# A fused transformer block: waits at the ramp, at the end of attention and in the last stage, and the order of the work around them

## The chip, the cores and the metric

The kernel runs on one core of one Trainium2 chip. The time is the device time of one execution in microseconds; three runs were made, and the median counts. The profile is of one execution of its own.

## The reference

One transformer block with its two branches in parallel, on x of 2048 tokens by 640 (float32). The normalised x feeds the windowed attention and the gated branch, and both are added to x.

```python
xn = layernorm(x)                                   # 2048 x 640
q, k, v = split(xn @ wqkv)                          # 32 heads of 20
scores = q @ k.T * 20 ** -0.5                       # only 0 <= query - key < 256
A = softmax(scores) @ v, heads joined, @ wo
B = (gelu(xn @ w_gate) * (xn @ w_up)) @ w_down      # 1728 wide
out = x + A + B
```

## The kernel before, in words

A product of two float32 matrices is made as three products of their rounded upper and lower parts (`h` and `l` in the names: xh, xl, wqh, wql). ScalarE copies the upper part, and VectorE or GpSimd subtracts it from the raw value for the lower part. A "dense" tile of 128 features by 512 tokens is so 15 matmuls of 128x128 by 512 columns (`dense_steps`, L106).

**Ramp.** Each of the four chunks of 512 tokens is normalised, transposed on TensorE (L184) and split into xh (ScalarE, L192) and xl (VectorE, L193). Before the last chunk's transposes are all copied out, attention's first maxima begin: `attention` (L802) runs twelve steps ahead of its first unit, which pull pairs of maxima on every second step and eight dense matmuls on each.

**Attention.** It goes over 32 units: a unit is four heads (a group) by one chunk of 512 queries, with 14 slots (`NS`) each. `max_pair` (L472, matmuls ps_m L491, row maxima on VectorE L501) finds the maxima that the softmax subtracts; it takes two PSUM banks of a pool of four, which the transposes of the ramp use too. `exp_piece` (L542) makes scores (ps_e, L556) and their exponentials P on ScalarE (L558), in six pairs on the odd slots 1 to 11. `clear` (L564) lets GpSimd zero the parts of P outside the window (the selects, L571 and L574). In slot 0 of the next unit `av_unit` (L577) multiplies P by V (ps_o, L599, 96 short matmuls in the trace), ScalarE copies the two halves out (L605, L606) and GpSimd adds them (L609). `load_stack` (L457) loads a unit's queries and keys (qs, ks, L466) from DRAM three units ahead.

Between these, TensorE gets dense matmuls from a generator, `filler` (L689): `pull_fill(n)` adds n to a debt and issues matmuls until it is paid. Each slot pulls RATE / NS. The generator goes through `sets` in their order: ("qk", i) is one weight tile for queries and one for keys for all four chunks, ("gu", f) one tile of gate and up; V of the second half of the heads comes in between at a given slot. Each q/k tile is saved in three bfloat16 parts with a step on ScalarE, VectorE and GpSimd (L276, L272, L254, L258) and stored to DRAM (L267).

```python
RATE = 31.2                                                              # L32
...
    sets = [("qk", 1), ("qk", 2), ("qk", 3), ("gu", 0), ("qk", 4)]       # L684
    sets += [("gu", f) for f in range(1, NFA)] + [("gu", NF - 1)]
...
        for u in range(NU + 1):                                          # attention
            for i in range(NS):
...
                if i == 0 and u:
                    av_unit(u - 1)
                    flush()
                    pull_max(2, T)
...
                pull_fill(RATE / NS)
```

**Gate phase.** The other tiles of gate and up (L864 `gate_up`, L931 `gate_up_pair`, ps_g L106 and L949) run on sums of two chunks, which need fewer products. `w_tiles` (L898) splits the weights, the lower parts on GpSimd (wql, L99 and L881).

**Last stage.** P is done; the down projection and the output projection run as eight pairs of 128 tokens (p), each of ten steps (k and "e"). In step n the program loads the activations of step n + 4 (`load_step`), splits those of step n + 2 (`split_step`, L1145: ScalarE L1162 and L1170, VectorE by the helper of L1054), does what `plan` has for n (`prepare`, L1402) and then issues the step's matmuls (ps, L1216, `terms`). In `plan`, "f" fetches a weight quad (on ScalarE's queue, L1020), "h" makes its upper part (ScalarE, L1035) and "l" its lower one (VectorE, L1054); "b" is a quad as it is, "t" one of sums. `drain` (L1234) adds finished PSUM banks into the output (xr, L1239).

**Order.** Each engine takes its instructions in order. In attention the order of TensorE, ScalarE, VectorE and GpSimd is the written one (`manual_schedule`), SyncE's is a scheduler's. In the gate phase (L1294) TensorE, ScalarE, VectorE and SyncE follow the written order, GpSimd the scheduler's. The last stage has all five written. Where two phases meet, the work of the later one can stand among that of the earlier one.

Of the kernel before, what the change touches and what calls it, by code (L numbers as in the profile page):

```python
# [28 lines left out]
SR = 3 * DH  # L29
QROWS = 64 + SR  # L30
NS = 14
RATE = 31.2  # L32
V1_SLOT = 169
MXD = 7
KSLOT = 9
# [9 lines left out]
RAMP = 4.0  # L45
GAP = 16
VW = 1408
MANUAL_OUT = {mybir.EngineType.SP}
MANUAL = {mybir.EngineType.PE, mybir.EngineType.Activation, mybir.EngineType.DVE}
# [17 lines left out]
def block_kernel(ctx, tc, x, wqk, wv, wgu, wdo, wdl, out):  # L67
# [129 lines left out]
    now = [None]  # L197

    def at(slot, fn, *a):
        acts.setdefault(slot, []).append((fn, a))  # L200
# [9 lines left out]
    def flush():  # L210
        while lates:
            fn, a = lates.pop(0)
            fn(*a)
# [4 lines left out]
    def defer(n, fn, *a):  # L218
        if now[0] is None:
            fn(*a)  # L220
        else:
            at(now[0] + n, fn, *a)
# [109 lines left out]
    def run(*gens):  # L332
        for gen in gens:
            for _ in gen:
                pass
# [121 lines left out]
    def load_stack(u, which=(0, 1)):  # L457
        g, c = divmod(u, NC)
        for m in range(80 * g // 128, (80 * g + 79) // 128 + 1):
            assert all((m + 5 * i, c) in done for i in which), (u, m)  # L460

        for i in which:
            dst, src, top, again = ((qs[u % NQ], qd[c], 1, 2), (ks[u % NK], kd[c], 0, 0))[i]
            for j in (0, 2):
                for p, part, n in ((j * 32, top, 2), (j * 32 + 2 * DH, again, 1), (64 - j * 32, 0, 3)):
                    nc.sync.dma_start(dst[p:p + DH * n, j:j + 2].rearrange("p j t -> p (j t)"),  # L466
                                      src[g, part:part + n].rearrange("s (d j) t -> (s d) (j t)",
                                                                      j=4)[:, j * C:(j + 2) * C])
# [54 lines left out]
    def pieces(c):  # L523
        b = 4 * c
        X = [(b, 0, 0, 384)] + ([(b - 2, 384, 0, 128)] if c else [])
        Y = [(b + 1, 0, 128, 384), (b + 3, 384, 384, 128)]
        Z = ([(b - 1, 0, 0, 256)] if c else []) + [(b + 2, 256, 256, 256)]
        return X, Z, Y
# [48 lines left out]
    def av_unit(u):  # L577
        g, c = divmod(u, NC)
        v = vtiles[g]
        os = [psx.tile([128, C], F32, name="ps_o", tag="ex") for _ in range(2)]  # L580
        place = {kb - 4 * c: (pts[u, bi], col, q0) for bi, bank in enumerate(pieces(c)) for kb, col, q0, n in bank}

        def half(d, r):
            i = 2 * d + r
            return d, r, max(0, 64 * i), min(C, 64 * i + 320)

        steps_ = [((0, 0), (0, 1)), ((2, 0), (-1, 1)), ((-1, 0), (2, 1)), ((1, 0), (1, 1)),
                  ((3, 0), (-2, 1)), ((-2, 0), (3, 1))]
        todo = [half(*x) for pair in steps_ for x in pair if x[0] in place]
        begun_, left = set(), [sum(t[1] == r for t in todo) for r in range(2)]  # L590
        for d, r, qa, qb in todo:
            pt, col, q0 = place[d]
            kb = 4 * c + d
            assert (id(v), kb) in done, (u, kb)
            left[r] -= 1
            rows = slice(64 * r, 64 * r + 64)
            for j in range(4):
                w0_ = kb * 84 + 21 * j
                nc.tensor.matmul(os[r][32 * j:32 * j + 32, qa:qb], v[rows, w0_:w0_ + 32],  # L599
                                 pt[rows, j, col + qa - q0:col + qb - q0], start=r not in begun_,  # L600
                                 stop=not left[r], skip_group_check=True, tile_position=(64 * r, 32 * j))
            begun_.add(r)
        ob, oc = ap.tile([128, C], F32, name="ob", tag="ob", bufs=1), pts[u, 2][:, 0]
        lo = 0 if c else 64
        nc.scalar.activation(ob, os[0], AF.Copy)  # L605
        nc.scalar.activation(oc[:, lo:], os[1][:, lo:], AF.Copy)  # L606

        def join():
            nc.gpsimd.tensor_tensor(out=ob[:, lo:], in0=ob[:, lo:], in1=oc[:, lo:], op=OP.add)  # L609

        def store():
            for j in range(4):
                nc.sync.dma_start(od[c].rearrange("(d h) t -> h d t", h=H)[4 * g + j], ob[32 * j:32 * j + DH, :])
            nc.sync.dma_start(sd[c][4 * g:4 * g + 4, :], ob[DH::32, :])

        defer(3, join)
        defer(5, store)
# [63 lines left out]
                                   lambda k: xh[:, k, cs], lambda k: xl[:, k, cs], KT)  # L681
            defer(1, *((late, c4) if i else (c1,)))

    sets = [("qk", 1), ("qk", 2), ("qk", 3), ("gu", 0), ("qk", 4)]  # L684
    sets += [("gu", f) for f in range(1, NFA)] + [("gu", NF - 1)]
    pools = (wp, None), (hp, 2)
    rest = []
# [91 lines left out]
    NU = NG * NC  # L779
    stream = ((u, i) for u in range(NU) for i in range(8))  # L780
    fill = filler()
    debt = [0.0]

    def pull_max(n, slot):
        for _ in range(n):
            x = next(stream, None)
            if x is None:
                return
            max_pair(*x)
            if x[1] == 7:  # L790
                at(slot + (MXD if slot >= 0 else 4), max_end, x[0])

    def tick():
        todo = [y for t in sorted(t for t in acts if t <= now[0]) for y in acts.pop(t)]
        return sorted(todo, key=lambda y: y[0] is max_end)

    def pull_fill(n):
        debt[0] += n
        while debt[0] > 0:
            debt[0] -= next(fill, 1.0)  # L800

    def attention():  # L802
        now[0] = -1
        load_stack(0)
        load_stack(1)
        load_stack(2)
        for i, (p, k, half) in enumerate((p, k, half) for p in range(NC // 2) for k in range(2) for half in range(2)):
            for j, fn in enumerate(x_sums(p, k, half)):
                m = 10 * i + j
                at(NS * (XS0 + m // XSN) + m % XSN, fn)  # L810
        for i in range(12):
            now[0] = i - 13
            for fn, a in tick():
                fn(*a)
            if i % 2 == 0:
                pull_max(2, now[0])
            flush()
            pull_fill(2 * RAMP)
        pull_fill(GAP)
        for u in range(NU + 1):  # L820
            for i in range(NS):
                T = now[0] = NS * u + i
                for fn, a in tick():
                    fn(*a)
                if i in (0, 5, 9) or T == 3:
                    pull_max(2, T)
                if i == 0 and u:
                    av_unit(u - 1)
                    flush()
                    pull_max(2, T)  # L830
                if i % 2 and i < 12 and u < NU:
                    exp_piece(u, i - 1)
                    if i == 1 and u:
                        pull_fill(1)
                        debt[0] -= 1
                    exp_piece(u, i)
                flush()
                if u + 3 < NU and i in (KSLOT, 12):
                    load_stack(u + 3, (int(i == KSLOT),))
                pull_fill(RATE / NS)  # L840
        while acts:
            now[0] += 1
            for fn, a in tick():
                fn(*a)
            flush()
        now[0] = None
        run(fill)
        assert not acts

    with tc.manual_schedule(engines=MANUAL | {mybir.EngineType.Pool}):  # L850
        attention()
# [439 lines left out]
        nc.sync.dma_start(t, x[256 * p:256 * p + 256].rearrange("(a p) d -> p a d", a=2))  # L1291
        return t

    order = tc.manual_schedule(engines=MANUAL_OUT | MANUAL)  # L1294
    order.__enter__()
    raws_w = load_gu(NFA)
    banks = [psg.tile([128, C], F32, name="ps_g", tag=f"g{i}") for i in range(4)]
# [34 lines left out]
    for j, f in enumerate(range(NFA, NF - 1)):  # L1332
# [50 lines left out]
        if not end:  # L1383
            w = nxt_w[0], sums
    order.__exit__(None, None, None)
    order = tc.manual_schedule(engines=MANUAL_OUT | MANUAL | {mybir.EngineType.Pool})
# [9 lines left out]

    plan = {1: "hb4 lb4", 2: "hb5 lb5", 3: "hb6 lb6 s4", 4: "fb7 ht4 lt4", 5: "fb8 s5", 6: "hb7 ht5 lb7 lt5",
            7: "ft6 ft8 hb8 lb8", 8: "ft7 ht6 lt6", 9: "ft0 ht8", 10: "lt8 ht7 lt7", 11: "ft1 ft2 ht0 lt0",
            12: "ft3 ht1 lt1", 15: "p20", 16: "p21", 17: "p22", 18: "p23", 22: "p30", 23: "p31", 25: "p32",
            26: "p33"}  # L1400

    def prepare(n):  # L1402
# [24 lines left out]
    for n, (p, k) in enumerate(steps):  # L1427
        i = n % (NQD + 1)
# [71 lines left out]
```

## Time and profile before

| | us |
|---|---|
| median of 3 runs | 1049.95 |
| lowest, highest run | 1048.82, 1053.6 |
| the profiled execution | 1055.0 |
| its span, first to last instruction | 1053.2 |

The profile is of one execution, so its durations are held against its own 1055.0. An engine's busy time counts its instructions and not the waits between them; PE is TensorE, PEld its weight loads, DVE VectorE, ACT ScalarE, POOL GpSimd, SP SyncE. A row of the timeline gives start and duration in us, engine, line, operation, output <- inputs, shape, count, and in brackets the idle time before it and what ended it. In rows of windows stands the granted clock of TensorE, 1.00 at full speed.

### The profile page before, as it was taken

The page shows a single profiled execution, that of the slowest core. Times are in us where ns is not written, and L with a number is a line of the kernel's source. Part 1 is how long each engine was busy: PE and PEld are TensorE (multiplying, and loading weights), DVE is VectorE, ACT ScalarE, POOL GpSimd, SP SyncE. Part 2 cuts the span into 40 slices and gives each one's busy share as a digit, 9 for nine tenths or more (in the row PEclk, how much of TensorE's full clock was granted, in tenths as well). Part 3 has the DMA queues.
Part 4 walks back from the last instruction along what each step waited for, and adds up shares of the span by engine and source line. Part 5 has one row for each costly group of instructions (what it writes and reads, how often), then busy time and mean ns, then how long its engine had stood idle before and what let it go on. Part 6 is the DMA issues. An engine that isn't in the chain of part 4 may idle for free.

```text
span 1053.2 us, 25694 instructions
## 1 busy us (share of the span) xinstructions
PE 1037.1 (98%) x9393; PEld 837.1 (79%) x9393; DVE 742.0 (70%) x2018; ACT 528.6 (50%) x1120; POOL 385.6 (37%) x622
## 2 busy tenths in 40 slices
PE   8999999999999999999999999999999999999998
PEld 8878666666787666666668888888888999999998
DVE  7845666667655676677736787776556869888887
ACT  4434766676666667666675232223324544343332
POOL 6021687979665767877460111101110000000000
PEclk9999999999999999999999999999999999999999
DMA  5543355555533344544125576762217874443333
GB/s 198 188 125 99 103 160 161 162 181 153 162 89 106 104 145 125 172 138 155 59 66 192 177 248 207 251 252 110 75 62 254 258 236 131 131 133 115 119 126 105
DMA packets 105192, 158.76 MB, mean 151 GB/s; under 512 B 15420, under 2 KB 60092, under 8 KB 105064
## 3 DMA queue, kind: packets, MB, share of 16 engines
q1 hardware_dynamic: 102680, 150.95, 44.3%
q10 hardware_dynamic: 2384, 6.16, 1.8%
q8 instruction: 74, 1.21, 0.5%
q14 instruction: 54, 0.44, 0.1%
HBM read 101.78 MB, written 54.92 MB: 149 GB/s over the span
## 4 chain that ended last, share of the span: by engine, by line
PE 84%; DVE 7%; DMA 3%; ACT 3%; issue 2%; POOL 1%; SPq 0%; ACTq 0%; DVEq 0%; POOLq 0%
PE ps_g L949 22%; PE ps_d L106 20%; PE ps L1216 16%; PE ps_e L556 8%; PE ps_v L106 6%; PE ps_o L599 5%; PE ps_m L491 4%; DVE junk L501 2%; PE ps_g L106 1%; DVE at L1054 1%; DVE ss L1054 1%; DMA stg<-wtd 1%; DVE wb L1054 1%; PE ps_t L184 1%; DMA qs<-qd 1%
## 5 line engine op out<-in xcount | busy, mean ns | idle before, releaser
L501 DVE CUSTOM_DVE_ANT_0 junk<-ps_m,mask 128x320 bf16<-128x320 f32 (+2 forms) x512 | 242.7, 474 | 132.5 <-PE ps_m L491 75.0
L558 ACT ACTIVATE P<-ps_e 128x512 f32<-128x512 f32 (+2 forms) x384 | 198.8, 571 | 62.1 <-PE ps_e L556 60.1
L1216 PE MATMUL ps<-wb,at 128*128 128x320 f32 x999 | 156.6, 309 | 1.5 <-DVE at L1054 1.4
L1216 PEld LDWEIGHTS ps<-wb,at 128*128 128x128 f32 x999 | 148.9, 188 | 2.4 <-DVE at L1054 1.9
L571 POOL TENSOR_SCALAR_AFFINE_SELECT P<-P 128x256 f32<-128x256 f32 (+1 forms) x192 | 95.4, 501 | 68.5 <-ACT P L558 65.6
L556 PE MATMUL ps_e<-qs,ks 124*128 124x128 bf16 (+2 forms) x704 | 119.0, 278 | 0.5
L106 PE MATMUL ps_d<-xh,wql 128*128 128x512 f32 x310 | 99.3, 424 | 0.0
L106 PE MATMUL ps_d<-xh,wqh 128*128 128x512 f32 x310 | 98.3, 422 | 0.0
L106 PE MATMUL ps_d<-xl,wqh 128*128 128x512 f32 x310 | 98.2, 420 | 0.0
L99 POOL TENSOR_TENSOR wql<-wr,wqh 128x640 fp32r<-128x640 f32 x12 | 19.2, 1607 | 196.1 <-PE ps_g L949 151.0
L1216 PE MATMUL ps<-wt,at 128*128 128x320 f32 x552 | 89.2, 310 | 0.8 <-DVE xr L1239 0.8
L556 PEld LDWEIGHTS <-ks 124*128 124x128 bf16 x704 | 49.6, 98 | 50.3 <-issue 35.3
L574 POOL TENSOR_SCALAR_AFFINE_SELECT P<-P 128x512 f32<-128x512 f32 (+1 forms) x144 | 78.6, 554 | 17.6 <-ACT P L558 15.8
L1216 PEld LDWEIGHTS ps<-wt,at 128*128 128x128 f32 x552 | 82.9, 188 | 1.3 <-DVE xr L1239 1.0
L1170 ACT ACTIVATE at<-ss 128x512 fp32r<-128x512 f32 x59 | 37.3, 632 | 88.1 <-DVE ss L1054 88.1
L599 PE MATMUL ps_o<-P,v 64*32 64x320 f32 (+4 forms) x2816 | 74.8, 347 | 1.7 <-POOL P L574 1.7
L258 POOL TENSOR_TENSOR pt<-r,pt 128x512 bf16<-128x512 f32 x40 | 46.8, 1169 | 70.1 <-ACT pt L254 61.7
L599 PEld LDWEIGHTS ps_o<-P,v 64*32 64x32 f32 x2816 | 50.7, 106 | 23.9 <-POOL P L574 1.6
L491 PE MATMUL ps_m<-ks,qs 60*64 60x320 bf16 (+3 forms) x1472 | 63.2, 260 | 3.8 <-DVE xl L193 1.1
L106 PEld LDWEIGHTS ps_d<-xh,wql 128*128 128x128 f32 x310 | 56.7, 191 | 10.2 <-issue 1.1
L106 PEld LDWEIGHTS ps_d<-xl,wqh 128*128 128x128 f32 x310 | 56.3, 190 | 9.9 <-issue 1.3
L106 PEld LDWEIGHTS ps_d<-xh,wqh 128*128 128x128 f32 x310 | 56.1, 190 | 9.9 <-issue 1.6
(195 smaller groups left out, 1940.8 us busy)
## 6 DMA issues: line engine op xcount, KB each, us to landing
hr<-hd SPq DMA_DIRECT2D x104, 128.0 KB
hd<-he SPq DMA_DIRECT2D x50, 256.0 KB
wr<-wgu SPq DMA_DIRECT2D x27, 320.0 KB
qs<-qd SPq DMA_DIRECT2D x64, 120.0 KB
ks<-kd SPq DMA_DIRECT2D x64, 120.0 KB
xi<-x SPq DMA_DIRECT2D x16, 320.0 KB
qs<-qd SPq DMA_DIRECT2D x64, 80.0 KB
ks<-kd SPq DMA_DIRECT2D x64, 80.0 KB
```

Source lines behind the costliest of these rows:

```text
L106: nc.tensor.matmul(ps, a(k), b(k), start=n == 0, stop=n == 3 * nk - 1)
L258: nc.gpsimd.tensor_tensor(out=pt[:, l, :], in0=r, in1=pt[:, 1, :], op=OP.subtract)
L491: nc.tensor.matmul(ps[64 * h:64 * h + 64, col:col + w], q[rows, j, q0:q0 + 64], ks_, start=True, stop=True, tile_position=(64 * r, 64 * h))
L501: nc.vector.tensor_tensor_reduce(out=junk[:, 0:n], in0=ps[:, 320 - n:320], in1=mask[:, 320 - n:320], scale=1.0, scalar=NEG, op0=OP.add, op ...
L556: nc.tensor.matmul(ps[:, col:col + n], k[0:QROWS, j, kc:kc + 128], q[0:QROWS, j, q0:q0 + n], start=True, stop=True)
L558: nc.scalar.activation(pt[:, j, lo:hi], ps[:, lo:hi], AF.Exp, scale=SCALE)
L571: nc.gpsimd.affine_select(out=a, in_=a, pattern=[[0, n], [1, 128]], compare_op=OP.is_ge, fill=0.0, base=0, channel_multiplier=-1)
L574: nc.gpsimd.affine_select(out=a, in_=a, pattern=[[0, n], [-1, 128]], compare_op=OP.is_ge, fill=0.0, base=-1, channel_multiplier=1)
L599: nc.tensor.matmul(os[r][32 * j:32 * j + 32, qa:qb], v[rows, w0_:w0_ + 32], pt[rows, j, col + qa - q0:col + qb - q0], start=r not in begun ...
L949: nc.tensor.matmul(ps, i, j, start=first and n == 0, stop=n == len(work) - 1, skip_group_check=True)
L1170: nc.scalar.activation(hi[:, 3:7], s, AF.Copy)
L1216: nc.tensor.matmul(ps[bank][:, 0:HD], *work[bank][j], start=bank not in begun, stop=final[p, bank] == n and j == len(work[bank]) - 1, skip ...
```

## The change

- In the ramp's first step the two pairs of maxima are pulled apart: the first pair, four of the step's eight dense matmuls, the second pair, the other four.
- RATE goes from 31.2 to 30.9, and ahead of the last P times V up to eight more dense matmuls (LAST) are pulled.
- ("qk", 4) comes before ("gu", 0) in the sets.
- In the gate phase GpSimd follows the written order too.
- In the last stage's plan the two parts of quad t1 ("ht1 lt1") move from step 12 to step 13.

```diff
--- before.py
+++ after.py
@@ -29,7 +29,8 @@
 SR = 3 * DH
 QROWS = 64 + SR
 NS = 14
-RATE = 31.2
+RATE = 30.9
+LAST = 8
 V1_SLOT = 169
 MXD = 7
 KSLOT = 9
@@ -681,7 +682,7 @@
                                    lambda k: xh[:, k, cs], lambda k: xl[:, k, cs], KT)
             defer(1, *((late, c4) if i else (c1,)))
 
-    sets = [("qk", 1), ("qk", 2), ("qk", 3), ("gu", 0), ("qk", 4)]
+    sets = [("qk", 1), ("qk", 2), ("qk", 3), ("qk", 4), ("gu", 0)]
     sets += [("gu", f) for f in range(1, NFA)] + [("gu", NF - 1)]
     pools = (wp, None), (hp, 2)
     rest = []
@@ -812,7 +813,12 @@
             now[0] = i - 13
             for fn, a in tick():
                 fn(*a)
-            if i % 2 == 0:
+            if i == 0:
+                pull_max(1, now[0])
+                pull_fill(RAMP)
+                pull_max(1, now[0])
+                debt[0] -= RAMP
+            elif i % 2 == 0:
                 pull_max(2, now[0])
             flush()
             pull_fill(2 * RAMP)
@@ -825,6 +831,8 @@
                 if i in (0, 5, 9) or T == 3:
                     pull_max(2, T)
                 if i == 0 and u:
+                    if u == NU:
+                        pull_fill(LAST)
                     av_unit(u - 1)
                     flush()
                     pull_max(2, T)
@@ -1291,7 +1299,7 @@
         nc.sync.dma_start(t, x[256 * p:256 * p + 256].rearrange("(a p) d -> p a d", a=2))
         return t
 
-    order = tc.manual_schedule(engines=MANUAL_OUT | MANUAL)
+    order = tc.manual_schedule(engines=MANUAL_OUT | MANUAL | {mybir.EngineType.Pool})
     order.__enter__()
     raws_w = load_gu(NFA)
     banks = [psg.tile([128, C], F32, name="ps_g", tag=f"g{i}") for i in range(4)]
@@ -1396,7 +1404,7 @@
 
     plan = {1: "hb4 lb4", 2: "hb5 lb5", 3: "hb6 lb6 s4", 4: "fb7 ht4 lt4", 5: "fb8 s5", 6: "hb7 ht5 lb7 lt5",
             7: "ft6 ft8 hb8 lb8", 8: "ft7 ht6 lt6", 9: "ft0 ht8", 10: "lt8 ht7 lt7", 11: "ft1 ft2 ht0 lt0",
-            12: "ft3 ht1 lt1", 15: "p20", 16: "p21", 17: "p22", 18: "p23", 22: "p30", 23: "p31", 25: "p32",
+            12: "ft3", 13: "ht1 lt1", 15: "p20", 16: "p21", 17: "p22", 18: "p23", 22: "p30", 23: "p31", 25: "p32",
             26: "p33"}
 
     def prepare(n):
```

## The prediction

> **What bounds the kernel now.** I read the page first (busy time, the chain that ended last), then the list of who made TensorE wait, then the timeline around each of those waits.
>
> ```profile
> span 1053.2 us, 25694 instructions
> ...
> PE 1037.1 (98%) x9393; PEld 837.1 (79%) x9393; DVE 742.0 (70%) x2018; ACT 528.6 (50%) x1120; POOL 385.6 (37%) x622
> ...
> PE 84%; DVE 7%; DMA 3%; ACT 3%; issue 2%; POOL 1%; SPq 0%; ACTq 0%; DVEq 0%; POOLq 0%
> ```
>
> TensorE is busy for 1037.1 of 1053.2 us, so all its gaps together are 16.1 us. The change removes no matmul (the dense matmuls of 512 columns in the attention program number 930 before and after), so it can gain only what stands in those gaps, or matmuls that ran slowly. The list of waits names them: engine and line, who ended the wait, us in total, times, longest.
>
> ```profile
> PE ps_o L599 <- POOL P L574: 1.7, 2, 1.1
> PE ps L1216 <- DVE at L1054: 1.4, 2, 1.1
> PE ps_m L491 <- DVE xl L193: 1.1, 1, 1.1
> PE ps_m L491 <- DMA qs<-qd: 0.9, 2, 0.4
> PE ps L1216 <- DVE xr L1239: 0.8, 1, 0.8
> ```
>
> Four of the five lie where the change works: line 3 in the ramp, line 1 at the last P times V, lines 2 and 5 in the last stage. Line 4 it does not touch.
>
> **The ramp: two pairs of maxima apart.** Rows of windows (PE, PEld, DVE, ACT, POOL busy, then granted clock, DMA share, GB/s) and of the timeline (start, duration):
>
> ```profile
> 61.21:64.63 3.42, 2.11 (x22) 1.35 (x21) 3.36 (x9) 2.17 (x5) 1.17 (x1) 1.00 0.46 138
> 64.63:68.04 3.41, 3.41 (x10) 2.67 (x9) 1.09 (x6) 0.00 (x0) 0.00 (x0) 0.50 0.70 218
> 545.91:549.33 3.42, 2.02 (x52) 1.20 (x52) 3.39 (x5) 0.67 (x2) 3.42 (x6) 1.00 0.46 149
> ...
> 61.13 3.19 DVE L193 TENSOR_TENSOR xl<-ps_t,xh 128x512 fp32r<-128x512 f32 x5
> 61.79 1.58 ACT L192 ACTIVATE xh<-ps_t 128x512 fp32r<-128x512 f32 x3
> 62.46 0.20 PE L491 MATMUL ps_m<-ks,qs 60*64 60x64 bf16 x1
> 63.77 0.31 PE L491 MATMUL ps_m<-ks,qs 60*64 60x64 bf16 x5 [1.11 <-DVE xl L193]
> 64.01 2.01 PE L106 MATMUL ps_d<-xh,wqh 128*128 128x512 f32 x5
> 69.14 0.39 PE L106 MATMUL ps_d<-xh,wqh 128*128 128x512 f32 x1
> ```
>
> The second pair waits 1.11 us for a PSUM bank of the transposes that VectorE's fourth xl frees (61.13 + 4 x 0.64 = 63.7). The built order of the changed kernel puts four dense matmuls between the pairs. They read xh of k = 0 to 3; the three ACT copies of 61.79 to 63.37 take 0.53 each, so k = 3 is there at 62.85, ahead of the fourth matmul. The step's eight fills are then four earlier and four later, none more. At 0.23 us each (five from 551.65 to 552.80, quoted below) the four fill 4 x 0.23 = **0.92 us** of the gap; what is late next is the same bank at 63.77, and 0.2 us of the wait stays.
>
> The second row is worth more. For 3.41 us after the thin window the granted clock is 0.50: the 15 dense matmuls from 64.01 to 69.14 take 5.13 us, where 15 x 0.23 is 3.45. That costs **1.68 us**. The thin window held transposes, 64-column matmuls and the gap; 0.92 us of full dense work inside it should keep the clock at 1.00. The bounds are 0 and 1.68. For the profiled execution I take 1.68, the value of the row itself; whether another execution has that loss at all, one trace cannot tell.
>
> The Trainium skill, "TensorE: Matmul & The Clock Gate" (sections "What's actually happening" and "Why this matters for your kernels"), says that the clock halves after an idle window of some 3.4 us and that gaps below about 3 us do no harm, the window running free of the kernel's start. The first row speaks against the harmless gap: TensorE was idle for 1.31 of 3.42 us, and half speed followed. The third row speaks for it: 1.40 us idle, and five matmuls soon after (551.65 to 552.80, below) ran at 0.23 each. By the page alone the four matmuls win 0.92 and no clock.
>
> **The end of attention: GpSimd's written order, eight matmuls, the rate.**
>
> ```profile
> 544.89 0.70 PE L556 MATMUL ps_e<-qs,ks 124*128 124x128 bf16 x4
> 546.24 2.02 PE L599 MATMUL ps_o<-P,v 64*32 64x320 f32 x52 [0.65 <-POOL P L574]
> 549.34 1.12 PE L599 MATMUL ps_o<-P,v 64*32 64x320 f32 x44 [1.08 <-POOL P L574]
> 551.65 1.31 PE L106 MATMUL ps_g<-xh,wql 128*128 128x512 f32 x5
> 552.80 0.39 PE L106 MATMUL ps_g<-xl,wqh 128*128 128x512 f32 x1
> ...
> 542.78 1.57 POOL L99 TENSOR_TENSOR wql<-wr,wqh 128x640 fp32r<-128x640 f32 x1 [0.32 <-ACT wqh L98]
> 546.19 0.87 POOL L571 TENSOR_SCALAR_AFFINE_SELECT P<-P 128x256 f32<-128x256 f32 x1
> 547.03 1.17 POOL L881 TENSOR_TENSOR wql<-wr,wqh 128x384 fp32r<-128x384 f32 x1
> 548.15 0.59 POOL L571 TENSOR_SCALAR_AFFINE_SELECT P<-P 128x256 f32<-128x256 f32 x1
> 549.24 0.59 POOL L571 TENSOR_SCALAR_AFFINE_SELECT P<-P 128x256 f32<-128x256 f32 x1
> ```
>
> Between the last scores (end 545.59) and the last P times V nothing is left to do, and GpSimd runs two weight differences of the next phase, 1.57 and 1.17 us, ahead of the selects that P needs. The waits are 0.65 + 1.08 = 1.73 us. The rate of 30.9 holds back 0.3 matmul per unit, 9.6 over 32 units, and LAST spends them: the built order has nine dense matmuls in that place where there were none, 9 x 0.23 = 2.07 us. They are moved, not added. In the new order the 1.17 us difference stands behind the selects, the 1.57 us one still ahead of the last three.
>
> The sum from 545.59: P times V starts at +2.07, its first part takes 2.02 and ends at +4.09. GpSimd: the earlier half's selects ended at 547.06 (+1.5) with the 1.57 us difference ahead of them, so without it between -0.1 and +1.5. I take the middle, +0.7. Then the difference ends at +2.3 and three selects of 0.59 at +2.9, +3.5 and +4.0. The second part waits for the middle one (L574 in its row), so 0.6 us is to spare and **1.73 us** go; without the nine matmuls it would be wanted at +2.0 and wait 1.5. From +1.5 the three selects end at +4.8 and 0.2 to 0.8 of a wait is left. Bounds: 0.9 and 1.73. The 1.17 us difference now goes ahead of the sum of the two halves of the output, which nothing reads before the last stage; the rest of GpSimd's order in the gate phase is the same as before.
>
> **The weight quad one step later.**
>
> ```profile
> 851.93 0.33 ACTq L1020 DMA_DIRECT2D stg<-wtd  x1
> 854.27 1.28 ACT L1035 ACTIVATE wt<-stg 128x1280 fp32r<-128x1280 f32 x1 [3.59 <-DMA stg<-wtd]
> 855.45 0.50 ACT L1162 ACTIVATE at<-hr 128x384 fp32r<-128x384 f32 x1
> ...
> 851.93 0.42 DVE L1054 TENSOR_TENSOR he<-hr,he 64x256 fp32r<-64x256 f32 x1
> 855.58 1.49 DVE L1054 TENSOR_TENSOR wt<-stg,wt 128x1280 fp32r<-128x1280 f32 x1 [3.23 <-ACT wt L1035]
> 856.99 0.42 DVE L1054 TENSOR_TENSOR ss<-hr 128x256 f32<-128x256 f32 x1
> 858.75 0.69 DVE L1054 TENSOR_TENSOR at<-ss,at 128x512 fp32r<-128x512 f32 x1 [0.23 <-ACT at L1170]
> 861.26 0.69 DVE L1054 TENSOR_TENSOR at<-ss,at 128x512 fp32r<-128x512 f32 x1 [0.23 <-ACT at L1170]
> ...
> 858.58 1.00 PE L1216 MATMUL ps<-wb,at 128*128 128x320 f32 x5 [1.05 <-DVE at L1054]
> 861.18 1.48 PE L1216 MATMUL ps<-wb,at 128*128 128x320 f32 x9
> 876.12 2.23 PE L1216 MATMUL ps<-wt,at 128*128 128x320 f32 x12 [0.77 <-DVE xr L1239]
> ```
>
> ScalarE's queue stands 3.59 us on the load of quad t1, and behind it the split of the next activations, VectorE's part of it and TensorE. With ht1 and lt1 behind that split, ScalarE is held only by ft3's issue (851.93, which stays at its step) and VectorE starts the split at 852.35. A split takes 2.45 us (856.99 to 859.44), so it is ready at 854.8 (its input had landed: in the trace it began as soon as both engines were free); TensorE wants it at 858.58 - 1.05 = 857.53. The wait of **1.05** goes. Late next: t1's own 1.28 and 1.49, from 854.27 to 857.07 as before, then the following split, ready at 859.5 instead of 861.95, wanted at about 860.6 (six of the nine matmuls of 861.18 are that step's, less 1.05). VectorE then runs 2.4 us earlier against TensorE's 1.05, so the later waits, 0.77 and the other 0.3 of the "at" line, shrink by up to 1.35. t1 itself is read more than ten steps on. Bounds 1.05 and 2.2; I take **2.0**, as VectorE has no idle stretch between them.
>
> **The swap of qk 4 and gu 0.** It moves eight differences of 1169 ns on GpSimd, and the stores of their eight tiles, some four units earlier.
>
> ```profile
> 150.00:250.00 100.00, 98.59 (x1307) 64.86 (x1298) 68.76 (x252) 68.33 (x142) 84.18 (x137) 1.00 0.57 168
> ...
> L258 POOL TENSOR_TENSOR pt<-r,pt 128x512 bf16<-128x512 f32 x40 | 46.8, 1169 | 70.1 <-ACT pt L254 61.7
> ```
>
> A stretch full of q/k projections has GpSimd at 84% and no wait of TensorE for it, so the swap is hidden; I allow 0 to +1.7 us (a second stall like line 4 of the waits, 0.9 us, in each of two units) and take 0.8 for it and the shifted queues. SyncE's queue otherwise only exchanges neighbours.
>
> **The sum.** For the profiled execution, 1055.0 us with what lies around its span: 0.92 + 1.68 + 1.73 + 2.0 - 0.8 = 5.5, so 1049.5. The median of the runs is 1049.95, 5.05 below that execution, so a median run may lack the half-clock loss; I count half of it, 0.84: 0.92 + 0.84 + 1.73 + 2.0 - 0.8 = 4.7, and the forecast is **1045.2 us**, own range 1043.7 to 1047.0. About 0.5% (5.2 us: below 1044.7 or above 1055.2) is what a measurement can tell from no change.
>
> **Rivals.** *All of it counts*: half clock in nearly every execution, the tail at 2.2, no new stall: 0.92 + 1.68 + 1.73 + 2.2 = 6.5, so 1043.4. For it: the row of 0.50; against: the profiled execution was a long one.
>
> *Given back*: the time won before the last stage is lost where DMA and VectorE set the pace, and only the quad counts, 1.05 to 2.0: 1048.4. For it: DVE and DMA are 10% of the chain; against: each of those waits is released by something TensorE started, and moves with it.
>
> *The clock does not hang on this gap*: half speed comes or stays away whatever stands between the pairs, so 0.92 + 1.73 + 2.0 - 0.8 = 3.9 and 1046.1. For it: the third window row, as idle as the first and followed by no half speed; against: the first. The Trainium skill's rule on gaps under 3 us (the page named above) comes to the same.
>
> *Slower: q loads late in every unit.* With less fill per unit and SyncE's queue shifted, the qs loads land after their maxima are due. The price is line 4's 0.9 per unit. It cancels the gain from six units on, and from twelve it is slower by over 0.5%; at all 28 units that load this way 28 x 0.9 = 25 us, 1070. Against it: it struck one unit of 28, and a unit becomes shorter by only 0.3 x 0.23 = 0.07 us.
>
> **Chances.** Forecast 0.43 (0.18 of it below 1044.7), all of it 0.2, the clock apart 0.12 (0.02 below), given back 0.18, slower 0.07. So faster by over 0.5%: 0.40; within: 0.54; slower: 0.06 (0.01 of the last rival stays within). The range of 1042.4 to 1050.0 takes in the first rival with 1 us below it (the lowest run was 1.1 below the median) and the one given back with two stalls.
>
> **What would show it.** Right: no wait of 1.11 near 63.8 and clock 1.00 after it; no PE wait for POOL before the last 96 matmuls of ps_o; no wait for "at" or "xr" near 858 and 876; line 4 unchanged. Wrong: half clock at another place, several ps_m waits for qs loads, or a TensorE wait in the last stage that wasn't there.

## The result and the profile after

| | before | after |
|---|---|---|
| median of 16 runs each, side by side, us | 1050.85 | 1047.49 |
| lowest, highest run, us | 1048.82, 1054.16 | 1045.18, 1050.52 |
| the profiled execution, us | 1055.0 | 1047.3 |
| its span, us | 1053.2 | 1045.6 |

The ratio is 0.9967, with a 95% interval of 0.9955 to 0.9979: 3.4 us less. Two later comparisons, with other runs of both kernels, gave 0.9949 (0.9934 to 0.9965) and 0.9954 (0.9936 to 0.9972), so 5.4 and 4.8 us less. The change is real, about 0.4%: none of the three intervals reaches 1. The two profiled executions are 7.7 us apart, more than twice as much; why is the main thing to learn here.

The page of the kernel after (busy time by engine; the chain that ended last by engine):

```profile
span 1045.6 us, 25699 instructions
...
PE 1033.1 (99%) x9393; PEld 835.1 (80%) x9393; DVE 743.2 (71%) x2018; ACT 527.8 (50%) x1120; POOL 384.5 (37%) x622
...
PE 94%; DVE 4%; ACT 1%; DMA 1%; issue 1%; SPq 0%; POOL 0%; DVEq 0%; ACTq 0%
```

TensorE's share of the chain rose from 84% to 94%, and of 16.1 us of gaps 12.5 are left. Of the waits of TensorE (us in total, times, longest), the five shown before are gone or down to 0.2. Two lead it now: one in the first stage, where the tokens load, and one that was 0.7 before:

```profile
PE ps_t L185 <- DVE xi L168: 3.0, 3, 1.7
PE ps_m L492 <- DVE mx L502: 1.5, 5, 0.4
```

(After the change the program's lines stand one to eight lower: L492 is the old L491, L600 the old L599.) Windows around the ramp and in the first stage of the kernel after, with the granted clock as the third number from the right:

```profile
61.21:64.63 3.42, 3.04 (x28) 2.07 (x27) 3.40 (x6) 2.60 (x6) 1.17 (x1) 1.00 0.46 138
64.63:68.04 3.41, 3.41 (x21) 2.39 (x21) 1.51 (x10) 0.60 (x1) 0.00 (x0) 1.00 0.76 224
10.85:14.26 3.41, 2.10 (x11) 1.51 (x12) 2.98 (x10) 3.08 (x10) 1.54 (x2) 1.00 0.72 281
14.26:17.67 3.41, 3.41 (x18) 3.41 (x17) 3.40 (x10) 1.92 (x5) 3.41 (x5) 0.50 0.21 53
```

The ramp's window holds 3.04 us of TensorE work instead of 2.11, and no 0.50 follows it. But a stretch at 0.50 still stands in the first stage, as it did before. Rows of the timeline of the kernel after:

```profile
62.71 1.17 PE L107 MATMUL ps_d<-xh,wqh 128*128 128x512 f32 x4
...
64.20 0.31 PE L492 MATMUL ps_m<-ks,qs 60*64 60x64 bf16 x5 [0.19 <-DVE xl L194]
...
448.07 0.29 PE L492 MATMUL ps_m<-ks,qs 60*64 60x320 bf16 x1 [0.23 <-DVE mx L502]
448.72 0.33 PE L492 MATMUL ps_m<-ks,qs 60*64 60x320 bf16 x3 [0.35 <-DVE mx L502]
...
542.56 1.29 PE L107 MATMUL ps_d<-xl,wqh 128*128 128x512 f32 x5
543.78 2.51 PE L600 MATMUL ps_o<-P,v 64*32 64x320 f32 x96
...
542.60 1.57 POOL L100 TENSOR_TENSOR wql<-wr,wqh 128x640 fp32r<-128x640 f32 x1
544.83 0.86 POOL L572 TENSOR_SCALAR_AFFINE_SELECT P<-P 128x256 f32<-128x256 f32 x1
545.66 1.17 POOL L889 TENSOR_TENSOR wql<-wr,wqh 128x384 fp32r<-128x384 f32 x1
...
847.71 1.26 ACT L1043 ACTIVATE wt<-stg 128x1280 fp32r<-128x1280 f32 x1
```

The four dense matmuls stand between the pairs, and 0.19 of 1.11 us is left. The last 96 matmuls of P times V run without a wait, and the 1.17 us difference stands behind the selects. ScalarE starts quad t1 (847.71) with no wait. New are waits for maxima in units 24 to 26 (434 to 464 us), two of which are shown.

Where the time went, from the starts of rows in each kernel's one profiled execution (ramp: first maximum to first P times V; attention: from there to the first ps_g; last stage: first ps to the end of the span; the last column gives when a stretch of 3.41 us at 0.50 began, the one that runs into the end of the span left out). The kernels are those of the next section.

| kernel | ramp | attention | last stage | 0.50 from |
|---|---|---|---|---|
| before | 45.87 | 443.11 | 244.10 | 13.4, 64.6 |
| pool | 45.88 | 442.08 | 243.26 | 13.5, 64.7 |
| ramp | 43.35 | 442.04 | 244.52 | 13.6 |
| last | 45.79 | 441.45 | 242.32 | 63.1 |
| quad | 44.27 | 442.11 | 241.34 | none |
| swap | 44.26 | 441.82 | 244.78 | none |
| rate312 | 43.36 | 443.08 | 241.89 | none |
| noramp | 44.18 | 441.90 | 240.95 | 13.6 |
| after | 43.25 | 441.13 | 240.62 | 14.3 |
| again | 43.28 | 441.86 | 242.45 | none |
| again2 | 43.26 | 441.19 | 242.54 | 13.1 |
| busy | 43.28 | 441.18 | 243.37 | none |
| fill12 | 43.27 | 441.69 | 241.88 | none |
| best | 43.35 | 441.82 | 243.52 | none |

Between before and after the three stages give 2.6 + 2.0 + 3.5 us, and the time up to the first maximum, 61.41 and then 61.84, takes 0.4 back. The gate phase took 258.5 to 258.7 in all fourteen.

### The profile page after: what moved, and what is told of

It is laid out like the page before. It is cut to its first block, busy times and chain, and to the rows that moved or that the text cites. A ratio compares the mean times of both kernels' runs of the same rounds, so it can differ in the third digit from the quotient of the medians.

```text
span 1045.6 us, 25699 instructions
## 1 busy us (share of the span) xinstructions
PE 1033.1 (99%) x9393; PEld 835.1 (80%) x9393; DVE 743.2 (71%) x2018; ACT 527.8 (50%) x1120; POOL 384.5 (37%) x622
## 4 chain that ended last, share of the span: by engine, by line
PE 94%; DVE 4%; ACT 1%; DMA 1%; issue 1%; SPq 0%; POOL 0%; DVEq 0%; ACTq 0%
PE ps_g L957 23%; PE ps L1224 23%; PE ps_d L107 20%; PE ps_e L557 8%; PE ps_v L107 6%; PE ps_o L600 5%; PE ps_m L492 5%; DVE junk L502 2%; PE ps_g L107 1%; DMA wr<-wqk 1%; PE ps_t L185 1%; PE ps_d L356 0%; DVE r L273 0%; DVE xl L194 0%; ACT P L559 0%
## 5 line engine op out<-in xcount | busy, mean ns | idle before, releaser
L575 POOL TENSOR_SCALAR_AFFINE_SELECT P<-P 128x512 f32<-128x512 f32 (+1 forms) x144 | 76.4, 538 | 16.3 <-ACT P L559 14.6
L600 PE MATMUL ps_o<-P,v 64*32 64x320 f32 (+4 forms) x2816 | 74.2, 347 | 0.0
L600 PEld LDWEIGHTS ps_o<-P,v 64*32 64x32 f32 x2816 | 50.9, 106 | 21.5 <-issue 0.9
L492 PE MATMUL ps_m<-ks,qs 60*64 60x320 bf16 (+3 forms) x1472 | 64.9, 260 | 3.1 <-DVE mx L502 1.5
L492 PEld LDWEIGHTS <-qs 60*64 60x64 bf16 x1472 | 29.2, 105 | 43.6 <-issue 38.0
```

Source lines behind the costliest of these rows:

```text
L492: nc.tensor.matmul(ps[64 * h:64 * h + 64, col:col + w], q[rows, j, q0:q0 + 64], ks_, start=True, stop=True, tile_position=(64 * r, 64 * h))
L575: nc.gpsimd.affine_select(out=a, in_=a, pattern=[[0, n], [-1, 128]], compare_op=OP.is_ge, fill=0.0, base=-1, channel_multiplier=1)
```

## The experiments

Four kernels that each do one part, on one chip beside the kernel before.

**ramp**: the kernel before with only the split of the first two pairs.

```diff
-            if i % 2 == 0:
+            if i == 0:
+                pull_max(1, now[0])
+                pull_fill(RAMP)
+                pull_max(1, now[0])
+                debt[0] -= RAMP
+            elif i % 2 == 0:
```

> The kernel before with the first two pairs of maxima apart, and nothing else. The prediction's term: the 1.11 us wait near 63.8 shrinks to about 0.2 (0.92 us won), and no granted clock of 0.50 follows it. Forecast: -0.9 us in an execution that had no half clock there, -2.6 in one that had it, so -1.8 in the median if half of the executions of the kernel before have it. Rival 'the clock does not hang on the gap': -0.9 us, and 0.50 still comes or stays away after 64.6 whatever stands there. Rival 'given back': the ramp is 2 us earlier at the 17th dense matmul and the start of the last stage is not earlier at all, 0 us.

Measured: 1050.03 us beside 1052.04, ratio 0.9983 (0.9971 to 0.9995): -1.8. Its windows, beside those of the run **last**, which has the pairs together, at the same work:

```profile
61.40:64.81 3.41, 3.03 (x25) 2.10 (x25) 3.35 (x9) 1.96 (x4) 1.17 (x1) 1.00 0.47 141
64.81:68.23 3.42, 3.42 (x22) 2.39 (x21) 1.55 (x8) 0.60 (x1) 0.00 (x0) 1.00 0.70 209
```

```profile
59.69:63.10 3.41, 2.10 (x22) 1.34 (x21) 3.35 (x8) 2.15 (x5) 1.16 (x1) 1.00 0.46 139
63.10:66.51 3.41, 3.41 (x10) 2.67 (x9) 1.10 (x6) 0.00 (x0) 0.00 (x0) 0.50 0.72 211
```

With the pairs together 0.50 followed in three of six executions (before, pool, last; not in quad, swap, noramp), and with four dense matmuls between them in none of eight. In the table the ramp takes 45.8 to 45.9 with it, 44.2 to 44.3 without, 43.3 with the dense matmuls: 1.6 for the clock, 0.9 for the gap. The runs without a profile bear this out. A stretch at 0.50 lowers a run's mean granted clock by 0.0016, to 0.998, and the 26 runs of the kernels busy, fill12 and best (below), which all have the split and a filled first stage, have 0.999 or 1.000. With the five other profiled ones that makes 31 executions with the split, and none had the ramp's half clock.

**last**: the rate, the eight matmuls and the exchange, without GpSimd's written order.

```diff
-RATE = 31.2
+RATE = 30.9
+LAST = 8
...
-    sets = [("qk", 1), ("qk", 2), ("qk", 3), ("gu", 0), ("qk", 4)]
+    sets = [("qk", 1), ("qk", 2), ("qk", 3), ("qk", 4), ("gu", 0)]
...
+                    if u == NU:
+                        pull_fill(LAST)
```

> The kernel before with the rate of 30.9, the eight dense matmuls ahead of the last P times V, and the exchange of qk 4 and gu 0 that the lower rate needs; GpSimd's order is left to the scheduler as before. The prediction's term: both waits for P at the last P times V go, -1.73 us (0.9 to 1.73), less up to 0.8 for the exchange, so -0.9 to -1.7. The prediction puts the moved 1.17 us weight difference down to GpSimd's written order: by that, without the written order the difference stays between the selects and 0.2 to 0.8 us of wait for P is left. The rival: the order comes out the same without it, no wait for P is left, and the written order does nothing.

Measured: 1050.28, ratio 0.9986 (0.9972 to 1.0): -1.5. No wait for P is left, and GpSimd's rows stand in the same order as in the kernel after: the rival's side. The written order is not what moves the 1.17 us difference. Its rows (the last select, the difference behind it, and the 96 matmuls without a wait):

```profile
544.69 2.50 PE L600 MATMUL ps_o<-P,v 64*32 64x320 f32 x96
...
545.73 0.85 POOL L572 TENSOR_SCALAR_AFFINE_SELECT P<-P 128x256 f32<-128x256 f32 x1
546.56 1.17 POOL L884 TENSOR_TENSOR wql<-wr,wqh 128x384 fp32r<-128x384 f32 x1
```

**quad**: only the plan's entry.

```diff
-            12: "ft3 ht1 lt1", 15: "p20",
+            12: "ft3", 13: "ht1 lt1", 15: "p20",
```

> The kernel before with ht1 and lt1 taken a step later, and nothing else. The prediction's term: -2.0 us (1.05 to 2.2): no waits for 'at' near 858 and for 'xr' near 876, the last stage shorter by that. The pair of traces so far shows the last stage 3.5 us shorter, so the rival is that the quad alone brings 3.5, and the term was too small. A second rival: the length of ScalarE's wait for the load of t1 (3.59 us in the trace of before) varies from execution to execution, the profiled one was long, and the median of the runs gets about 1 us.

Measured: 1050.15, ratio 0.9982 (0.9966 to 0.9998): -1.9. In its trace the waits at 858 and 876 are gone and one of 0.33 (before also there) is left. The second rival is half borne out: the load's length does vary, but the profiled one was not long, and the gain of 1.9 lies nearer the term's 2.0 than its 1 (the interval, 0.2 to 3.6 us, holds both). ScalarE's row for t1 in four executions of the old order, ramp, swap, pool and last, and then in quad (start, duration, wait and what ended it):

```profile
851.03 1.27 ACT L1040 ACTIVATE wt<-stg 128x1280 fp32r<-128x1280 f32 x1 [4.16 <-DMA stg<-wtd]
```

```profile
850.20 1.28 ACT L1035 ACTIVATE wt<-stg 128x1280 fp32r<-128x1280 f32 x1 [4.50 <-DMA stg<-wtd]
```

```profile
852.42 1.27 ACT L1035 ACTIVATE wt<-stg 128x1280 fp32r<-128x1280 f32 x1 [2.92 <-DMA stg<-wtd]
```

```profile
849.20 1.28 ACT L1038 ACTIVATE wt<-stg 128x1280 fp32r<-128x1280 f32 x1 [1.87 <-DMA stg<-wtd]
```

```profile
849.12 1.26 ACT L1035 ACTIVATE wt<-stg 128x1280 fp32r<-128x1280 f32 x1
```

With 3.59 in the kernel before, which is the middle of the five, the load cost 1.87 to 4.50 us of ScalarE's time, and TensorE's wait for "at" near 858 was 0, 0.20, 1.05, 1.44 and 1.71, in the order of ScalarE's 1.87, 2.92, 3.59, 4.16 and 4.50. A step later ScalarE mostly finds it landed: no wait, or 0.13 us, in six of the nine executions with the moved quad, 0.35, 0.80 and 0.98 in the other three, and TensorE has no wait there in any. The wait for xr near 876 is less regular: 0.65 to 0.77 in the five executions of the old order, and in the nine of the new one none in six, but 0.22, 0.34 and 0.65 in rate312, again and busy.

**swap**: only the exchange in the sets (its two lines are shown above).

> The kernel before with qk 4 ahead of gu 0, and nothing else. The prediction allows 0 to +1.7 us (took 0.8) as a hidden move of GpSimd's differences and of the stores. If it is hidden, the time is within 0.3 us of the kernel before and the waits of TensorE between 100 and 540 are the same; if not, new waits for qs or for a maximum stand there, 0.9 us each.

Measured: 1051.31, ratio 0.9991 (0.9975 to 1.0007): no difference that can be told. No new wait stands between 100 and 540. But the exchange is no free extra either: without it, by the program's order and not by a run, the rate of 30.9 leaves the first chunk of qk 4 unfinished when unit 24's load of it is due.

Then four in a second comparison: **again** is the changed kernel itself.

> The changed kernel once more, beside the next three, with the kernel before on the same chip. If the first comparison (-3.4 us, interval -4.7 to -2.2) was right, the difference lies in that interval again. The parts measured alone came to -1.8 (ramp), -1.5 (rate, eight matmuls and exchange, without GpSimd's written order) and -1.9 (quad), -5.2 together; if they add, this run shows about -5.

Measured: 1047.19 beside 1051.86, ratio 0.9949 (0.9934 to 0.9965). The parts (-1.8, -1.5, -1.9) add to -5.2, which it meets.

**pool**: the kernel before with only GpSimd's written order.

```diff
-    order = tc.manual_schedule(engines=MANUAL_OUT | MANUAL)
+    order = tc.manual_schedule(engines=MANUAL_OUT | MANUAL | {mybir.EngineType.Pool})
```

> The kernel before with GpSimd in written order in the gate phase, and nothing else. The built order is the same on all five engines as that of the kernel before, so the expectation is 0 us; it is a second sample of the kernel before, and its trace shows which waits and which intervals at granted clock 0.50 differ from one execution to the next. The prediction's step (the written order moves the 1.17 us difference behind the selects) expects one of the two waits for P, 1.08 us, to be gone.

Measured: 1051.18, ratio 0.9999 (0.9981 to 1.0017). Both waits for P are there, 0.65 and 1.08. The edit does nothing here: in the two traces each engine's instructions stand in the same order. As a second sample of the kernel before, its profiled execution has no wait for qs loads at all, where the first had 0.85 us.

**rate312**: the changed kernel, the rate back at 31.2.

> The changed kernel with the rate back at 31.2: by its built order no dense matmul is left for the place ahead of the last P times V (nine in the changed kernel). Theory: the two waits for P come back (0.65 and 1.08 listed, 2.2 to 2.4 in time, as each wait costs some 0.25 more than the list shows), and the waits for maxima near 435 to 465, which the changed kernel and the run with rate 30.9 alone have (1.1 listed, some 1 us in time over units 24 and 25), go: the difference is +1.2 against the changed kernel. Rival: the lower rate is worth its whole 1.73 and nothing comes back: +1.7 to +2.3. Second rival: it is worth nothing, 0.

Measured: 1049.41, 2.2 more than again (ratio to the kernel before 0.9973, 0.9957 to 0.9988). Its timeline:

```profile
542.99 2.02 PE L600 MATMUL ps_o<-P,v 64*32 64x320 f32 x52 [0.65 <-POOL P L575]
546.10 1.12 PE L600 MATMUL ps_o<-P,v 64*32 64x320 f32 x44 [1.08 <-POOL P L575]
...
543.78 1.17 POOL L889 TENSOR_TENSOR wql<-wr,wqh 128x384 fp32r<-128x384 f32 x1
544.91 0.59 POOL L572 TENSOR_SCALAR_AFFINE_SELECT P<-P 128x256 f32<-128x256 f32 x1
545.46 0.59 POOL L575 TENSOR_SCALAR_AFFINE_SELECT P<-P 128x256 f32<-128x256 f32 x1
```

With GpSimd's order written and no dense matmul held back, the 1.17 us difference stands ahead of three selects again. So it is the count of dense matmuls that decides where the next phase's weight differences stand among the selects. The waits for maxima near 435 to 465 are gone. Against again the median comes nearer to the first rival (+1.7 to +2.3) than to the theory's +1.2, but the interval of each ratio is some 3 us wide. The traces settle more: both executions have 0.85 us of waits for qs loads, and attention takes 443.08 and 441.86, a difference of 1.2, the theory's figure.

**busy**: more matmuls of the zero tile in the first stage.

```diff
-WARM = 64
+WARM = 74
...
             part(dn[1], wh5, xh, halves[0], True)
+            for i in range(12):
+                nc.tensor.matmul(dn[1][:, 256:384], warm, warm, start=False, stop=False, skip_group_check=True)
```

> The changed kernel with more idle-time matmuls in the first stage: 74 matmuls of the zero tile ahead of the first transposes where there were 64, and 12 more (adding zeros to the second half of the second sum, before its own products) in the 0.75 us wait near 13.6 us. Theory: the clock is judged over fixed stretches of 3.41 us whose place differs from execution to execution, and a stretch with too few rows streamed is followed by one at 0.50; by an estimate from the rows of six traces, stretches beginning between 9.3 and 10.5 us are thin enough, a third of the places. Filled, the 0.50 near 10 to 18 us comes in no execution: no run below clock 0.999 but for the stretch at the end, and the mean falls by 1.68 us x the share of executions that had it (9 of the changed kernel's 16 runs showed 0.997 or 0.998), so -0.6 to -1.0 against the changed kernel, its lowest run unchanged. Rival: half speed comes whatever stands there: as many runs at 0.997 and 0.998 as before, and the time is the same or 0.3 longer.

Measured: 1047.20 beside again's 1047.19 (ratio to the kernel before 0.9958, 0.9943 to 0.9973). The clock's part came as the theory has it: all 12 runs have a mean granted clock of 0.999 or 1.000, where of the changed kernel's 34 runs in three comparisons 16 have 0.998 or 0.997. The time did not follow. The traces show part of the reason: from the start to the first maximum busy takes 60.26 us, against 59.79 in again, which had no 0.50 either, and 61.13 and 61.84 in again2 and after, which had it. By these rows the filling gains about 1.6 where the clock would have halved, and costs about 0.5 (60.26 - 59.79, one execution each): as an estimate 1.6 x 16/34 - 0.5 = 0.3 is left, too little to be seen.

Last, four in one comparison: **again2** is the changed kernel once more, **noramp** it without the split, **fill12** it with only the twelve zero matmuls (the second hunk above), **best** the same with RATE = 31.05.

> The changed kernel a third time, as the baseline for the three beside it: -3.4 to -5.4 us against the kernel before, the two results so far.

> The changed kernel with the first two pairs of maxima together again. By the prediction's terms +0.92 for the gap, and +0.84 for the clock (half of the executions): +1.8. By the theory of fixed stretches of 3.41 us, from the traces: the gap costs 0.84 in time (2.52 between the two traces less 1.68 for one stretch at 0.50), and a third of the places of such a stretch (beginnings from 60.6 to 61.6 us, 1.0 of 3.41) give a half-clock stretch worth 1.68, so 0.84 + 0.5 = +1.3; more runs at 0.996 and 0.997. Rival 'the clock does not hang on the gap': +0.84.

> The changed kernel with only the twelve zero matmuls in the 0.75 us wait near 13.6 us (64 in front as before). Stretches beginning from 9.3 to 10.5 us are no longer thin, some beginning near 5 to 7 us can be: runs at 0.997 and 0.998 become fewer (9 of 16 and 4 of 12 for the changed kernel) without being gone, and the mean falls by 1.68 us x the difference of these shares, some 0.3 to 0.7. Rival: what the twelve add on TensorE (12 x 0.05 us) takes it back: 0.

> The same with a rate of 31.05 instead of 30.9: by its built order five dense matmuls lie ahead of the last P times V instead of nine, and the dense matmuls between the maxima of units 24 and 25 shift by one. If the waits for maxima near 435 to 465 hang on that, some 1.0 us goes, and a wait for P of about 0.9 comes back: -0.5 to +0.5 against the run before. If they hang on the lower rate in another way, they stay and it is +0.9.

Measured: again2 1047.60 (0.9954), noramp 1048.74 (0.9968, 0.9953 to 0.9983), fill12 1047.34 (0.9950, 0.9932 to 0.9968; 5 runs), best 1048.65 (0.9958, 0.9943 to 0.9973). noramp is 1.1 above again2, between the rival's 0.84 and the 1.3 of fixed stretches; the medians can't tell these apart. Its window beside the same stretch of swap, both followed by full clock at the same gap of 1.1 us:

```profile
61.42:64.83 3.41, 2.11 (x20) 1.47 (x21) 3.31 (x9) 1.89 (x4) 1.16 (x1) 1.00 0.46 138
64.83:68.24 3.41, 3.41 (x23) 2.35 (x21) 0.86 (x4) 0.50 (x1) 0.00 (x0) 1.00 0.70 203
```

```profile
60.02:63.43 3.41, 2.11 (x17) 1.54 (x16) 3.21 (x10) 1.71 (x4) 1.17 (x1) 1.00 0.45 137
63.43:66.84 3.41, 3.41 (x22) 2.41 (x21) 0.80 (x4) 0.60 (x1) 0.00 (x0) 1.00 0.71 205
```

fill12 kept its runs at 0.999 and 1.000 and close together (1046.26 to 1047.55), but it is not shown to be faster than the changed kernel. best missed what was expected of it: with five dense matmuls no wait for P came back, and the waits for maxima did not go, they moved to 389 to 405. In means it is 1.1 above fill12 (1048.23 against 1047.13); in the two profiled executions, 1.5 apart, the last stage alone differs by 1.6 (243.52 against 241.88), and the edit does not touch it. So no run shows a version that beats the changed kernel.

## Why the prediction was right, and where its steps were not

The forecast was 1045.2 us, a change of -4.7 from a median of 1049.95. Three comparisons gave -3.4, -5.4 and -4.8, and the medians after were 1047.49, 1047.19 and 1047.60, inside the range of 1042.4 to 1050.0. They are 2.0 to 2.4 above the forecast. Of the first comparison's 2.3, 0.9 is the base (1050.85, where the forecast had 1049.95) and the other 1.4 a smaller change; in the two others the change was as large as forecast or larger, and the base, 1051.86 and 1052.86, makes the difference. Within 0.5% was the likeliest class, and the first comparison's -0.33% lies in it. The rival "given back", by which only the quad counts, falls: ramp and last gained 1.8 and 1.5 without it. "All of it counts", 6.5, is more than any of the three shows.

By the table, with the mean of the executions that have a part and of those that have it not:

| term | forecast | by the traces |
|---|---|---|
| gap in the ramp | 0.92 | 0.9 |
| half clock after it, halved | 0.84 | 1.6 x 3/6 = 0.8 |
| end of attention, with the exchange | 1.73 - 0.8 = 0.93 | 442.37 - 441.49 = 0.9 |
| weight quad | 2.0 | 243.80 - 242.06 = 1.7 |
| sum | 4.7 | 4.3 |

**Ramp.** Both terms held. To count the clock for half was a guess from the profiled execution's length, and it came out near: the stretches of 3.41 us lie elsewhere in each execution, and three of six had it. More runs give a little less: the mean granted clock is 0.9982 over 85 runs of the kernel before and 0.9989 over 57 runs with the split and no filling, and at 0.0016 for one stretch that is, as an estimate, 0.4 of the executions. The rival by which the clock does not hang on the gap falls (three of six against none of 31). The Trainium skill, "TensorE: Matmul & The Clock Gate" (section "What's actually happening"), says that the window of 3413 ns runs free of the kernel's start; the rows agree, since 13.43 and 64.63 of the kernel before lie fifteen stretches of 3.413 apart, and other executions have other starts. Its section "Why this matters for your kernels" warns of idle gaps above about 3 us; here 1.3 us of idle time in one stretch were followed by half clock in before, pool and last, and by full clock in swap and noramp.

**End of attention.** The net was right and three steps under it were wrong. First, GpSimd's written order was given the moved difference: pool, last and rate312 show that it moves nothing, the held-back matmuls do. Second, the exchange was called a hidden move with a price of 0.8: it costs nothing that is seen, and is what makes the lower rate possible. Third, the matmuls held back were taken to be missed nowhere: in units 24 to 26 there are now four waits for maxima (0.26, 0.23, 0.35 and 0.26 us in the kernel after). They replace most of what the waits for P gave. So 1.73 was too much and 0.8 the wrong deduction, and the two errors cancelled, which is luck. Why the maxima come late in just those units is open.

**Weight quad.** The mechanism (ScalarE's queue stands on a load, VectorE and TensorE behind it) is shown by five load waits in order with five waits of TensorE. The step that fails is that 1.05 was read as a fixed price: it was 0 to 1.71, with a mean of 0.88. In the profiled pair the last stage gained 3.48, over the bound of 2.2, because listed idle time is not the whole cost (below), and later the average gained 1.7. Also unseen: in five of the nine executions with the moved quad a wait for xr stands near 837 to 839, up to 1.56 us in again2, where ScalarE waited for the load of an earlier quad:

```profile
835.07 1.27 ACT L1043 ACTIVATE wt<-stg 128x1280 fp32r<-128x1280 f32 x1 [2.16 <-DMA stg<-wtd]
```

In none of the five with the old plan is it there. In noramp ScalarE waited 1.41 there, for VectorE, and in the kernel after 1.37 for a load, and TensorE not at all. The moved quad cannot cause it by its place in the order: in before and quad every engine's instructions stand in the same order up to ScalarE's part of t1, some 10 us later. What brings it is open.

**Line 4, the qs loads.** "Unchanged" was wrong, but the slower rival was too. The waits vary from 0 to 1.0 us between executions (0.85, 0, 0, 0, 0 and 0.85 at the rate of 31.2; 0.2 to 1.0 in all seven at 30.9), and strike two units at most. Whether the lower rate makes them likelier is open.

**The signs named.** No 1.11 wait and full clock after the ramp, no wait for P: all seen. No wait for "at" or "xr" in the last stage: so in the kernel's first trace, not in again (0.34 for each, near 869 and 875).

## What to carry to other kernels

Split what one trace shows into waits that the order of work makes, which come in each execution, and those that a load's landing or the place of a clock stretch makes, which vary; a forecast for the median takes the former whole and the latter by their share of executions. A part that is thought to be free (an order that is written out, an exchange) is worth one run alone, since here the one did nothing and the other was what the lower rate needed. Dense work that is saved up for a known gap is missed where it came from, so look for the place at which the other engine sets the pace next.

## What the runs showed of the hardware

A wait cost TensorE more here than its listed idle time. In the last stage forty matmuls ps take 5.87 us from start to start; the forty with the listed wait of 1.05 in the kernel before took 7.18, so 1.31, the next disturbed groups 7.27 (0.11 and 0.77 idle) and 6.66 (0.33 idle). That is 3.5 together where the idle times add to 2.26, and the whole of the last stage's 3.48 in the profiled pair.

Busy time does not tell which stretch is followed by half clock: 2.10 to 2.12 us of TensorE was followed by 0.50 in last and pool and by 1.00 in swap and noramp. An estimate of the streaming time sorts the ramp's stretches better: each matmul that begins in the stretch, counted with the usual distance between starts of its kind, 0.23 us for a dense one (0.12 at 256 columns) and 0.11 for a transpose. Before, pool and last have three dense ones and four or five transposes, 1.1 to 1.2 us or 0.33 to 0.36 of the stretch, and half clock followed. Noramp has four and four (0.40), swap five and four (0.47) and quad none and fourteen (0.45), and full clock followed. In the first stage, counted in the same way, 0.35 to 0.38 was followed by 0.50, and 0.39 or more was not. The short matmuls of P times V do not fit it (an estimate of 0.1 at 546 in the kernel before, and full clock after it). It is a sorting of fourteen traces and no shown rule.
